# Linear attention and a routed attention layer on one core: the sums over phi(k) taken from three VectorE additions per pair of heads to two, with the rest of them on the array, and the order drawn up anew

## The chip, the cores and the metric

The kernel runs on one core of one Trainium2 chip. The core has five engines that run in parallel, each through its own list of instructions in order: TensorE (PE, with its weight loads PEld), VectorE (DVE), ScalarE (ACT), GpSimd (POOL) and SyncE (SP), which issues nearly all DMAs. The metric is the device time of one execution in microseconds; before the change it is 621.88 us (median of 3 runs, 620.62 to 622.17).

## What is computed

The reference is a linear attention, whose output goes through a layer that routes each token to two of four causal attentions:

```python
def phi(x):
    proj = np.einsum('bhsd,df->bhsf', x, w_phi)
    proj = proj - np.max(np.abs(proj), axis=-1, keepdims=True)
    return np.concatenate([np.exp(proj), np.exp(-proj)], axis=-1)
q_p, k_p = (phi(q), phi(k))
kv = np.einsum('bhsf,bhsd->bhfd', k_p, v)
z = np.sum(k_p, axis=2)
num = np.einsum('bhsf,bhfd->bhsd', q_p, kv)
den = np.einsum('bhsf,bhf->bhs', q_p, z)[..., None] + 1e-06
return (num / den)
...
for e in range(E):          # 4 experts, head size 64, S = 576, 2 of 4 per token
    q = x @ wq[e]; k = x @ wk[e]; v = x @ wv[e]
    ...                     # causal softmax a of q k^T / 8
    out += mask * w * ((a @ v) @ wo[e])
```

There are 8 batches, 8 heads, 576 positions, head size 64 and 128 features (256 with both signs). The change touches z, the sum of phi(k) over the 576 positions.

## The kernel before, in words

The work goes by **pairs** of heads, 32 of them (four to a batch), and by batches for the routed layer. For a pair, the k projection (`stream_k`, L509, nine matmuls, array in two halves of 64 rows) leaves nine blocks of 128 positions by 128 features in PSUM: four whole chunks of each head, and one block that holds the last 64 positions of both. `center` takes the maximum of each position on VectorE (L564) and subtracts it into the tile `ek` (L578); ScalarE makes the exponentials of both signs (L326). `ek` is then 128 positions x 2 signs x 9 blocks x 128 features.

`stream_kv` multiplies phi(k) with v (L605, twenty f32 matmuls, the array in four column tiles of 32, four at a time) and then makes z in the same PSUM tile (L622): a matmul whose weights are ones adds a block of phi(k) up over its positions. For the four pairs of the first batch all five blocks of a head go to the array. For the other 28 pairs `key_sum` (L542) first adds the four whole chunks of each head on VectorE, in three additions of 512 columns (L546), each of them over both signs and both heads, into the tile `zs` (128 x 2 signs x 2 heads x 128); the array then takes `zs` with ones (one round of four matmuls, 2 heads x 2 signs) and the shared block with `sel` (another round).

On the other side, `stream_q` projects q (L509), ScalarE copies the result out (u, L324), GpSimd takes the maximum over features (L681), VectorE subtracts it (L685), ScalarE makes both exponentials. `stream_n` makes the denominators (L710) and numerators (L721), `divide` the quotients x in two parts xh and xl (L753, L324, L319). When a batch's four pairs are through, `stream_s` projects queries and keys of the experts (L315, qk), makes scores (L838), GpSimd masks (L942) and takes maxima (L959), VectorE subtracts (L963), ScalarE exponentiates; `stream_v` makes values and gates (L315 vg, L924), `sums` the softmax denominators (L1001), `attend` the weighted values (L1030), `project_out` the output (L315 wo), which leaves through two tiles `ot` and a store per tile.

Nothing of this order is left to the hardware. Every step is a generator that says which engine it wants and what it needs; the loop of `Plan` picks at each moment the step with the lowest position among those that could start within WINDOW of the earliest, with positions from the tables MOVE, POS1, POS and BOFF, and costs for engines that could take a copy (`copies`, FLEX). Each engine's list is fixed by that. PSUM is eight tiles of 128 x 512 in one pool. While nothing is due at the start, TensorE is given matmuls on a constant tile (`warm`).

The lines that matter below: KADD (L46) is the number of VectorE additions' form; L544 to L551 are the two forms; L610 to L622 let the array take one partial sum per head and sign (`first` = 1) or two.

## Time and profile before

| what | value |
|---|---|
| median of 3 runs | 621.88 us (620.62 to 622.17) |
| the profiled execution's own time | 620.78 us |
| its span, first to last instruction | 619.0 us |
| PE / PEld busy | 607.7 us (98%) / 477.7 us (77%) |
| DVE busy | 541.4 us (87%), 1115 instructions |
| ACT busy | 424.2 us (69%), 1011 instructions |
| POOL busy | 246.0 us (40%) |
| mean granted TensorE clock | 0.998 |

The profiled execution is one run of its own: 1.8 us of its time lie outside the span, and it is 1.1 us below the median of the three runs. "Busy" of PE counts matmuls until their modelled ends, which overlap the next ones. Engines not named in the table (SP, the DMA queues) only move data.

### The profile page before, as it was taken

Reading aid. Unit: us, or ns where it says so; the run is one execution under the profiler, and the core shown is the slowest. Engines: PE = TensorE matmul, PEld = TensorE weight load, DVE = VectorE, ACT = ScalarE, POOL = GpSimd, SP = SyncE. Lnnn points to the kernel's source line nnn. Section 1 sums busy time; section 2 is a strip of 40 time slices with the busy share of each in tenths; the row PEclk is TensorE's granted clock in tenths of the full one; section 3 lists DMA queues with packets and bytes.
Section 4 is the critical chain, followed back from the end, with each engine's and each line's share of the span. In section 5 each row is a group of like instructions: output and inputs, shape, how many; then the busy total and the mean of one; then the engine's idle time right before and its main releaser. Section 6 shows DMA issues by size and latency. Waiting matters only on the chain.

```text
span 619.0 us, 20200 instructions
## 1 busy us (share of the span) xinstructions
PE 607.7 (98%) x8391; PEld 477.7 (77%) x8391; DVE 541.4 (87%) x1115; ACT 424.2 (69%) x1011; POOL 246.0 (40%) x167
## 2 busy tenths in 40 slices
PE   8999999999999999999999999999999999999996
PEld 7656888677896779767886778876789678877985
DVE  5899989999989997989999998789995899976693
ACT  4997769379565796569766867565867478753562
POOL 5644352284332644253445223345152336320520
PEclk9999999999999999999999999999999999999999
DMA  8653214333133431351314242144222311020012
GB/s 219 168 137 95 64 36 122 85 105 87 46 107 90 116 90 33 93 155 55 90 52 140 66 143 62 41 138 119 59 70 92 82 47 28 21 84 2 1 60 96
DMA packets 41611, 52.50 MB, mean 85 GB/s; under 512 B 21168, under 2 KB 24624, under 8 KB 41520
## 3 DMA queue, kind: packets, MB, share of 16 engines
q1 hardware_dynamic: 41200, 50.62, 28.1%
q8 instruction: 66, 1.08, 0.7%
q10 hardware_dynamic: 320, 0.59, 0.4%
q14 instruction: 25, 0.20, 0.1%
HBM read 36.64 MB, written 14.55 MB: 83 GB/s over the span
## 4 chain that ended last, share of the span: by engine, by line
PE 77%; DVE 11%; ACT 9%; issue 1%; DMA 1%; ACTq 0%; DVEq 0%
PE ps_c L315 32%; PE ps_c L605 9%; PE ps_c L509 9%; PE ps_c L721 7%; PE ps_c L1030 6%; PE ps_c L838 5%; PE ps_c L1001 3%; PE ps_c L710 3%; PE ps_c L622 2%; DVE zs L546 2%; ACT ek L326 2%; ACT u L324 2%; ACT mx L326 1%; DVE u L685 1%; DVE top L955 1%
## 5 line engine op out<-in xcount | busy, mean ns | idle before, releaser
L681 POOL PARTITION_ALL_REDUCE mx<-u x64 | 143.7, 2288 | 191.6 <-ACT u L324 188.7
L315 PE MATMUL ps_c<-xh,qk 128*128 128x320 f32 (+1 forms) x512 | 106.5, 299 | 1.8 <-DVE xl L319 1.0
L315 PEld LDWEIGHTS ps_c<-xh,qk 128*128 128x128 f32 x512 | 82.8, 188 | 4.4 <-DVE xl L319 1.2
L959 POOL PARTITION_ALL_REDUCE max<-top x16 | 58.8, 3676 | 67.8 <-DVE top L955 61.3
L942 POOL TENSOR_SCALAR_AFFINE_SELECT s<-s 128x256 f32<-128x256 f32 (+1 forms) x80 | 44.4, 590 | 89.8 <-ACT s L324 89.4
L326 ACT ACTIVATE ek<-ek 128x1152 f32<-128x1152 f32 x64 | 74.8, 1168 | 7.0 <-DVE ek L578 6.3
L605 PE MATMUL ps_c<-ek,v_in 128*32 128x256 f32 x1280 | 75.4, 380 | 0.9 <-ACT ek L326 0.9
L315 PE MATMUL ps_c<-xl,qk 128*128 128x256 f32 (+1 forms) x256 | 75.6, 295 | 0.0
L963 DVE TENSOR_TENSOR s<-s,max 128x1152 f32<-128x1152 f32 (+4 forms) x80 | 68.2, 880 | 4.9 <-POOL max L959 4.9
L685 DVE TENSOR_TENSOR u<-u,mx 128x576 f32<-128x576 f32 x64 | 60.9, 959 | 2.2 <-POOL mx L681 2.2
L605 PEld LDWEIGHTS ps_c<-ek,v_in 128*32 128x32 f32 x1280 | 40.2, 110 | 28.4 <-ACT ek L326 1.2
L315 PE MATMUL ps_c<-vg,xh 128*128 128x260 f32 (+1 forms) x320 | 59.0, 285 | 0.2 <-ACT s L324 0.2
L326 ACT ACTIVATE s<-s 128x1152 f32<-128x1152 f32 (+4 forms) x80 | 56.3, 739 | 3.6 <-DVE s L963 3.4
L564 DVE TENSOR_REDUCE pmax<-ps_c 128x4 f32<-128x512 f32 (+1 forms) x96 | 49.7, 542 | 8.2 <-PE ps_c L509 7.9
L324 ACT COPY s<-ps_c 128x512 f32<-128x512 f32 (+4 forms) x136 | 48.0, 460 | 8.9 <-PE ps_c L838 8.9
L315 PE MATMUL ps_c<-yh,wo 128*128 128x320 f32 (+1 forms) x256 | 52.8, 301 | 0.0
L324 ACT COPY u<-ps_c 128x320 f32<-128x320 f32 (+1 forms) x126 | 41.3, 411 | 15.6 <-PE ps_c L509 15.3
L326 ACT ACTIVATE mx<-u 128x576 f32<-128x576 f32 x64 | 44.0, 689 | 10.2 <-DVE u L685 10.0
L578 DVE TENSOR_TENSOR ek<-ps_c,pmax 128x512 f32<-128x512 f32 (+1 forms) x96 | 50.3, 540 | 0.2 <-PE ps_c L605 0.2
L315 PEld LDWEIGHTS ps_c<-vg,xh 128*128 128x128 f32 (+1 forms) x320 | 47.5, 177 | 1.3 <-ACT s L324 0.5
L315 PEld LDWEIGHTS ps_c<-xl,qk 128*128 128x128 f32 x256 | 48.2, 188 | 0.0
L509 PEld LDWEIGHTS ps_c<-wf,k_in 64*128 64x128 f32 x576 | 41.7, 191 | 8.0 <-DVE u L336 1.0
(119 smaller groups left out, 1379.3 us busy)
## 6 DMA issues: line engine op xcount, KB each, us to landing
v_in<-in_v_dram SPq DMA_DIRECT2D x32, 320.0 KB, 3.0
out_dram<-ot SPq DMA_DIRECT2D x32, 288.0 KB, 2.1
q_in<-in_qt_dram SPq DMA_DIRECT2D x60, 144.0 KB, 2.9
kvd<-kvt SPq DMA_DIRECT2D x104, 48.0 KB, 1.9
kv<-kvd SPq DMA_DIRECT2D x26, 192.0 KB, 2.5
k_in<-in_kt_dram SPq DMA_DIRECT2D x32, 144.0 KB, 2.8
k_in<-in_kt_dram SPq DMA_DIRECT2D x32, 128.0 KB, 2.7
q_in<-in_qt_dram ACTq DMA_DIRECT2D x4, 144.0 KB, 3.7
```

What stands on the lines that cost most here:

```text
L315: nc.tensor.matmul(o, a, b, start=start, stop=stop, skip_group_check=True)
L324: nc.scalar.copy(o, i)
L326: nc.scalar.activation(o, i, func, **kw)
L509: nc.tensor.matmul(o, a, b, start=True, stop=True, skip_group_check=True)
L564: dve(n * 128, [mk], [pk]).tensor_reduce(out=m[:, us], in_=src, axis=AX.X, op=ALU.max, apply_absolute_value=True)
L578: dve(n * 128, [e1k], [pk, mk]).tensor_tensor(out=ek2[p % EKB][:, 1, us, :], in0=src, in1=m[:, us].unsqueeze(2).to_broadcast([128, n, 128] ...
L605: nc.tensor.matmul(o[g, 0:2], v_in[:, 4 * h + t if t < 4 else 8 + h, k:64:2], ek[:, :, u_, :].rearrange("p c (w f) -> p c w f", w=4), star ...
L681: nc.gpsimd.partition_all_reduce(M, U, 128, bass_isa.ReduceOp.absmax)
L685: (nc.gpsimd if st.eng == 'POOL' else nc.vector).tensor_tensor(out=U, in0=U, in1=M, op=ALU.subtract)
L942: nc.gpsimd.affine_select(out=d, in_=d, pattern=[[0, 2], [1, w]], compare_op=ALU.is_ge, fill=FILL, base=0, channel_multiplier=-1)
L959: nc.gpsimd.partition_all_reduce(big.rearrange("p e s -> p (e s)"), top.rearrange("p e s -> p (e s)"), 128, bass_isa.ReduceOp.max)
L963: dve(2 * (S - 128 * j), [('d', x, j)], [('max', z)], 1.11, True).tensor_tensor(out=block(s_, j, None, rows(j)), in0=block(s_, j, None, ro ...
```

## The change

It sets KADD from 3 to 1, so that the second form of `key_sum` is used: for each sign one addition of 512 columns, chunks 0 and 1 of both heads plus chunks 2 and 3, into `zs` of twice the size; two additions per pair in place of three, and neither needs the other. The array takes two rounds of ones in place of one, and the `sel` round as before. All numbers that set the order and the choice of engine for a copy are other ones, too; a line of each kind stands here for the tables.

```diff
-HOT = 16.28
-SLOPE = (-37.28, -27.25, 9.68, 3.86, -6.2)
+HOT = 26.86
+SLOPE = (-74.83, -35.32, -26.8, 10.28, 10.22)
...
-KADD = 3
+KADD = 1
...
-FLEX = (447, -293)
+FLEX = (341, -272)
...
-WINDOW = 52.0
-SWITCH = 22.0
+WINDOW = 236.0
+SWITCH = 55.0
...
-ZEROS = 25.27
+ZEROS = 59.21
...
-BOFF = (-2.11, 8.18, 6.82, 2.05, 1.07, 6.82, 22.72, -5.5)
+BOFF = (-13.16, -1.84, 3.91, 19.47, 4.04, -0.92, 16.38, -56.14)
...
-OTHER = 12.77
+OTHER = 19.72
```

Two lines of the planner (in `key_sum` and `phi_q`) add FLEX[1] to a cost of GpSimd; they concern KPOOL and PSUB, which are 0 in both, so they change nothing.

The code that KADD picks, the same in both files:

```python
for a in range(1, 4 if KADD == 3 else 1):
    ...tensor_tensor(out=zs, in0=zs if a > 1 else x[:, :, :, 0], in1=x[:, :, :, a], op=ALU.add)
for c in range(0 if KADD == 3 else 2):
    ...tensor_tensor(out=zs[:, c], in0=x[:, c, :, 0:2], in1=x[:, c, :, 2:4], op=ALU.add)
```

How the order moves, at three places. The **key sum**, on TensorE, at the pair 17 (`ek` and `v_in` are its phi(k) and v; a row that ends in x20 stands for twenty matmuls). Before:

```order
L710 MATMUL ps_c_68<-u_132,kv_120 32x288
L605 MATMUL ps_c_70<-ek_109,v_in_107 32x2x4x32 x20
L622 MATMUL ps_c_70<-zs,ones 32x4x32 x4
L622 MATMUL ps_c_70<-ek_109,sel 32x4x32 x4
L721 MATMUL ps_c_67<-mx_139,kv_120 32x256 x2
L721 MATMUL ps_c_67<-mx_140,kv_120 32x256 x2
```
With the change:

```order
L710 MATMUL ps_c_66<-u_126,kv_119 32x288
L605 MATMUL ps_c_68<-ek_109,v_in_107 32x2x4x32 x20
L622 MATMUL ps_c_68<-zs,ones 32x4x32 x8
L622 MATMUL ps_c_68<-ek_109,sel 32x4x32 x4
L721 MATMUL ps_c_67<-mx_133,kv_119 32x256 x2
L721 MATMUL ps_c_67<-mx_134,kv_119 32x256 x2
```
The round of ones over `zs` has become two rounds; it still stands right behind the product with v. The same sum on VectorE, at the pair 4, the first that has one. Before:

```order
L753 TENSOR_TENSOR ps_c_65<-ps_c_65,xf 128x256
L753 TENSOR_TENSOR ps_c_68<-ps_c_68,xf 128x320
L546 TENSOR_TENSOR zs<-ek_108 128x512
L546 TENSOR_TENSOR zs<-zs,ek_108 128x512 x2
L319 TENSOR_TENSOR xl_148<-ps_c_65,xh_147 128x256
L319 TENSOR_TENSOR xl_148<-ps_c_68,xh_147 128x320
```
With the change:

```order
L336 COPY kvt<-ps_c_65 128x384
L551 TENSOR_TENSOR zs<-ek_108 128x512
L753 TENSOR_TENSOR ps_c_66<-ps_c_66,xf 128x256
L551 TENSOR_TENSOR zs<-ek_108 128x512
L319 TENSOR_TENSOR xl_146<-ps_c_66,xh_145 128x256
L753 TENSOR_TENSOR ps_c_63<-ps_c_63,xf 128x320
```
Three additions have become two, and a step of another kind stands between them.

The **start**, on ScalarE (`ek_108` is phi(k) of the first pair, `mx` and `u` are phi(q), `qk` a weight). Before:

```order
L324 COPY u_128<-ps_c_66 128x320
L326 ACTIVATE mx_134<-u_126 128x576
L326 ACTIVATE ek_108<-ek_108 128x1152 x2
L326 ACTIVATE mx_133<-u_125 128x576
L326 ACTIVATE mx_136<-u_128 128x576
L326 ACTIVATE u_128<-u_128 128x576
L324 CAST qk<-top_155 128x1152
L326 ACTIVATE u_125<-u_125 128x576
```
With the change:

```order
L324 COPY u_128<-ps_c_66 128x320
L326 ACTIVATE ek_108<-ek_108 128x1152 x2
L326 ACTIVATE mx_134<-u_126 128x576
L326 ACTIVATE u_126<-u_126 128x576
L326 ACTIVATE mx_135<-u_127 128x576
L326 ACTIVATE u_127<-u_127 128x576
L326 ACTIVATE ek_109<-ek_109 128x1152
L324 COPY kvt<-ps_c_66 128x384
```
The first pair's two exponentials of k come ahead of any of q; before, one of q stood ahead of them. On TensorE, 51 matmuls on the constant tile stand ahead of the second k projection in place of 75, and 87 in all in place of 117.

The **tail**, on ScalarE (the copies of the last batch's output tiles; `ot_171` takes the tiles 0 and 2, `ot_172` the tiles 1 and 3). Before:

```order
L324 CAST yh_169<-ps_c_64 128x320
L324 COPY ot_171<-ps_c_68 128x256
L324 COPY ot_171<-ps_c_70 128x320
L324 COPY ot_172<-ps_c_66 128x256
L324 COPY ot_172<-ps_c_64 128x320
L324 COPY ot_171<-ps_c_67 128x256
L324 COPY ot_172<-ps_c_65 128x256
```
With the change:

```order
L324 CAST yh_169<-ps_c_64 128x320
L324 COPY ot_171<-ps_c_69 128x256
L324 COPY ot_172<-ps_c_68 128x256
L324 COPY ot_171<-ps_c_67 128x320
L324 COPY ot_172<-ps_c_66 128x320
L324 COPY ot_171<-ps_c_65 128x320
L324 COPY ot_172<-ps_c_63 128x256
```
The first two tiles are now filled in turns, their first parts before their second ones; VectorE has the two other copies in both, the 320 of tiles 2 and 3 before, the 256 of tile 2 and the 320 of tile 3 now.

Over the whole lists, TensorE has 28 rounds of four matmuls more (112 instructions) and changes the shape of its array tiles 154 times in place of 164. VectorE loses 28 additions and gains 16 copies out of PSUM or of weights that ScalarE had; ScalarE loses these 16.

## Rows read from the trace of the kernel before

**Rows 1.** The page of the profile: its first line, the busy time of the engines over the whole span (microseconds, share of the span, instructions), and the shares by engine of the chain of work that ended last.
```profile
span 619.0 us, 20200 instructions
...
PE 607.7 (98%) x8391; PEld 477.7 (77%) x8391; DVE 541.4 (87%) x1115; ACT 424.2 (69%) x1011; POOL 246.0 (40%) x167
...
PE 77%; DVE 11%; ACT 9%; issue 1%; DMA 1%; ACTq 0%; DVEq 0%
```

**Rows 2.** Busy time of each engine in three stretches (start and end in us from the span's start, length, then busy us of each engine with its instructions, granted TensorE clock as a share of full speed, DMA share, GB/s): the ramp of the first batch, the middle, the last two batches and the tail.
```profile
0.00:62.00 62.00, 58.92 (x886) 40.72 (x888) 52.60 (x109) 49.19 (x99) 31.91 (x21) 1.00 0.58 155
62.00:530.00 468.00, 464.92 (x6433) 365.77 (x6433) 426.76 (x870) 327.80 (x780) 192.52 (x128) 1.00 0.29 83
530.00:619.00 89.00, 83.84 (x1084) 71.17 (x1075) 62.08 (x137) 47.22 (x133) 21.58 (x19) 0.99 0.13 46
```

**Rows 3.** The TensorE timeline around one pair's key sum (start us, us until the modelled end of the last one, engine, line, operation, out<-in, array tile, shape, records; an f32 matmul leaves two records, so x8 is one round of four).
```profile
101.74 0.43 PE L622 MATMUL ps_c<-zs,ones 128*32 128x128 f32 x8
101.98 0.40 PE L622 MATMUL ps_c<-ek,sel 128*32 128x128 f32 x8
102.20 1.54 PE L1001 MATMUL ps_c<-s,ones 128*32 128x288 f32 x40
```

**Rows 4.** Groups of instructions with shapes kept apart (line, engine, operation, out<-in, shapes, count; busy us, mean ns of one; idle us of the engine just before them and what ended it): the key sum's additions, a copy of VectorE out of PSUM, and the steps between a k projection and its exponentials.
```profile
L546 DVE TENSOR_TENSOR zs<-zs,ek 128x512 f32<-128x512 f32 x56 | 43.8, 783 | 0.9
...
L546 DVE TENSOR_TENSOR zs<-ek 128x512 f32<-128x512 f32 x28 | 21.2, 757 | 2.5 <-PE ps_c L622 1.5 <-ACT ek L326 0.9
...
L336 DVE COPY ot<-ps_c 128x320 f32<-128x320 f32 x13 | 6.4, 489 | 11.1 <-DMA out_dram<-ot 8.3 <-PE ps_c L315 2.2 <-ACT ps_c L326 0.5
...
L578 DVE TENSOR_TENSOR ek<-ps_c,pmax 128x512 f32<-128x512 f32 x64 | 41.8, 674 | 0.2 <-PE ps_c L605 0.2
...
L564 DVE TENSOR_REDUCE pmax<-ps_c 128x4 f32<-128x512 f32 x64 | 41.4, 675 | 8.2 <-PE ps_c L509 7.9
...
L326 ACT ACTIVATE ek<-ek 128x1152 f32<-128x1152 f32 x64 | 74.8, 1168 | 7.0 <-DVE ek L578 6.3
```

**Rows 5.** The TensorE timeline in two places (columns as in rows 3): the second round of L710 followed by a step of another tile shape, and followed by one of the same.
```profile
23.33 0.67 PE L710 MATMUL ps_c<-u,kv 128*32 128x288 f32 x8
...
23.93 0.38 PE L509 MATMUL ps_c<-wf,k_in 64*128 64x128 f32 x2
...
111.01 0.67 PE L710 MATMUL ps_c<-u,kv 128*32 128x288 f32 x8
...
111.49 0.38 PE L605 MATMUL ps_c<-ek,v_in 128*32 128x256 f32 x1
```

**Rows 6.** The start: rows of the timelines of TensorE, of VectorE and of ScalarE (columns as in rows 3; in brackets the idle time before the row and what ended it).
```profile
10.23 4.36 PE L315 MATMUL ps_c<-warm 128*128 128x128 bf16 x75
...
14.52 1.39 PE L509 MATMUL ps_c<-wf,k_in 64*128 64x128 f32 x18
...
16.28 2.37 PE L605 MATMUL ps_c<-ek,v_in 128*32 128x256 f32 x40
...
11.72 0.75 DVE L685 TENSOR_TENSOR u<-u,mx 128x576 f32<-128x576 f32 x1
...
12.39 0.28 DVE L578 TENSOR_TENSOR ek<-ps_c,pmax 128x128 f32<-128x128 f32 x1
...
12.50 0.68 ACT L326 ACTIVATE mx<-u 128x576 f32<-128x576 f32 x1 [1.40 <-DVE u L685]
...
13.09 2.34 ACT L326 ACTIVATE ek<-ek 128x1152 f32<-128x1152 f32 x2
```

**Rows 7.** The tail: rows of the timelines of TensorE, of VectorE and of ScalarE, and last one piece of the chain of work that ended last (start us, us, what).
```profile
608.45 0.46 PE L315 MATMUL ps_c<-yh,wo 128*128 128x320 f32 x2
...
608.89 0.40 PE L315 MATMUL ps_c<-yh,wo 128*128 128x256 f32 x2
...
609.25 0.45 PE L315 MATMUL ps_c<-yh,wo 128*128 128x320 f32 x2
...
609.59 0.49 DVE L319 TENSOR_TENSOR yl<-ps_c,yh 128x320 fp32r<-128x320 f32 x1 [0.49 <-ACT yh L324]
...
615.21 0.49 DVE L336 COPY ot<-ps_c 128x320 f32<-128x320 f32 x1 [0.36 <-DMA out_dram<-ot]
...
611.25 1.66 ACT L324 COPY ot<-ps_c 128x256 f32<-128x256 f32 x4 [1.69 <-PE ps_c L315]
...
615.13 0.37 ACT L324 COPY ot<-ps_c 128x256 f32<-128x256 f32 x1 [0.42 <-DMA out_dram<-ot]
...
612.93 2.10 DMA out_dram<-ot
```

**Rows 8.** Waits of TensorE's weight loads from 20 to 606 us (engine, out and line, what was waited for: us in total, times, longest us).
```profile
PEld ps_c L315 <- DVE xl L319: 1.6, 2, 1.2
...
PEld ps_c L509 <- DVE ps_c L753: 1.4, 3, 0.5
...
PEld ps_c L509 <- ACT mx L326: 1.4, 4, 0.5
...
PEld ps_c L605 <- ACT ek L326: 1.2, 2, 1.1
```

**Rows 9.** The TensorE timeline of the fourth pair: its k projection, and the step that multiplies its phi(k) with v (columns as in rows 3).
```profile
36.58 1.39 PE L509 MATMUL ps_c<-wf,k_in 64*128 64x128 f32 x18
...
45.60 0.64 PE L605 MATMUL ps_c<-ek,v_in 128*32 128x256 f32 x8 [0.86 <-ACT ek L326]
```

More of the change, by code (lines that the diff above doesn't have):

```diff
@@ L91 @@
-POS1 = {'wq': 7.17, 'wv': 21.48, 'wo': 24.58, 'n0': -30.0, 'n1': 2.78, 'k': -0.6, 'q': -13.78, 'v': -0.62, 'kv': -23.5, 'z': 3.8, 'cen': -4.87, 'evu': -35.73, 'ph0': 17.23, 'ph1': 17.65, 'div': -1.88, 'evd': -4.7, 'lk': -16.22, 'lq': 24.67}
-BOFF = (-2.11, 8.18, 6.82, 2.05, 1.07, 6.82, 22.72, -5.5)
-POS = {'fin': 39.8, 'p0': -3.53, 'p1': -40.28, 'v0': 21.78, 'gate': -24.77, 's0': -7.94, 's1': -10.44, 'm0': 9.16, 'm1': 14.32, 't0': -27.77, 't1': 0.1, 'out': 21.12}
[10 rows of a table added]
+    'evu': (6.8, -21.35, 6.41, -12.3, 7.4, 4.82, 5.05, -0.04, 5.64, -5.01, 5.49, 0.81, -18, -5.64, -22.38, 32.72, 17.12, -0.64, 33.16, 0.57, 12.47, -7.98, 2.62, -2.4, -19.71, 6.85, 3.73, 18.44, -22.69, 4.87, 5.04, -8.19,),
@@ new lines @@
+    'ph0': (12.06, 7.25, 8.9, -8.48, 13.11, 3.32, 23.51, 1.63, 5.19, 11.75, 1.44, 8.87, 7.87, 7.86, 11.54, 0.87, 4.08, -7.89, -0.79, -9.77, -9.31, 16.55, 14.79, 11.86, 9.9, 18.66, 2.49, -3.93, -11.7, -2.14, -14.68, 3.55,),
+    'ph1': (-7.2, -5.86, 14.43, 15.66, 0.79, -6.91, -0.21, 34.16, -10.58, 14.08, -26.56, -3.97, 5.79, -11.42, -2.79, 10.67, -6.73, 1.11, 5.61, -9.25, 2.64, -19.41, 6.71, 7.18, 1.87, 1.45, 1.84, 9.05, -0.28, 4.61, 5.76, -20.17,),
+    'cen': (-1.2, 3.62, -17, 0.94, -20.47, -6.74, 12.4, 4.64, -21.77, -36.49, -10.6, -25.81, -4.54, 6.27, -0.76, -1.9, 2.73, 13.05, 2.8, 9.13, -4.33, 10.79, 7.22, 12.38, 5.9, 11.33, -17.03, 22.59, -14.89, 15.82, -5.18, -7.13,),
@@ new lines @@
+    'evd': (0.41, 19.08, 30.39, 1.01, -20.32, -6.41, -5.63, -1.44, -15.71, 10, 2.66, -3.13, -0.96, 11.86, 4.83, -20.58, 5.65, 3.13, -3.27, -13, -2.84, 29.11, 23.04, 12.83, 0.44, 6.26, -11.11, 5.77, 11.32, 6.98, 0.21, 3.72,),
+    'n1': (3.76, -5.22, -7.46, 11.91, -10.85, 11.23, -18.4, 15.11, 1.37, -11.71, -10.88, -34.34, -3.24, -5.5, 15.08, -3.48, -14.77, -7.9, 5.38, 4.69, 14.84, -19.32, 19.63, 2.43, -13.85, 1.6, -11.58, 0.76, 2.28, -11.93, -16.19, -8.16,),
+    'div': (-8.63, 10.36, 12.6, 18.11, 18.3, -14.25, 5.79, -11.2, 13.01, -0.95, 14.74, -1.86, -16.45, -1.7, -11.92, 0.01, 20.01, 8.27, -10.23, -14.06, 22.17, 1.47, -24.38, 7.08, -1.85, 1.44, -5.84, 6.27, 5.79, -4.31, -7.71, -22.39,),
[6 rows of a table added]
@@ new lines @@
+    'gate': (31.69, -9.55, 4.05, -17.81, 18.54, 8.24, -6.2, 2.69,),
+    't1': (5.02, -0.41, 3, -7.78, 9.18, 15.59, -16.96, -12.72,),
+    'out': (12.41, 3.63, 9.76, 4.79, -6.99, 6.66, -2.08, -6.03,),
+    'fin': (0, 0, 0, 0, 0, 0, 0, -8.63,),
+}
+POS1 = {'wq': 50.59, 'wv': 25.6, 'wo': 36.27, 'n0': -37.41, 'n1': -2.16, 'k': 5.88, 'q': -19.68, 'v': -2.9, 'kv': -22.69, 'z': -14.51, 'cen': -33.17, 'evu': -85.86, 'ph0': 14.95, 'ph1': 12.23, 'div': -32.98, 'evd': -15.7, 'lk': -14.98, 'lq': 23.34}
+BOFF = (-13.16, -1.84, 3.91, 19.47, 4.04, -0.92, 16.38, -56.14)
@@ L95 @@
+POS = {'fin': 20.1, 'p0': 11.95, 'p1': -47.3, 'v0': 19.99, 'gate': -9.45, 's0': 11.63, 's1': 1.85, 'm0': 35.05, 'm1': 7.89, 't0': -12.14, 't1': 0.91, 'out': 23.79}
 NPAIRS = B * NP
@@ L547, in key_sum @@
         for c in range(0 if KADD == 3 else 2):
-            st = Step((('POOL', KPOOL), ('DVE', 65 + 1.11 * 512)) if KPOOL else 'DVE', ekk, pred=has('kv', p - 1) if p else None, port=True)
+            st = Step((('POOL', KPOOL + FLEX[1]), ('DVE', 65 + 1.11 * 512)) if KPOOL else 'DVE', ekk, pred=has('kv', p - 1) if p else None, port=True)
             yield st
```

13 lines of the change are left out of this document (1 added, 12 removed), and 32 rows, old and new, of the table MOVE.

## The prediction

> **What bounds the kernel now.** I read the page first. TensorE is busy for 607.7 of 619.0 us and 77% of the chain that ended last runs over it; VectorE follows with 87% busy and 11% of the chain [rows 1]. A share of busy time alone proves little, so I cut the span into stretches. In the middle, from 62 to 530 us, TensorE shows 464.9 busy of 468 us, at the full granted clock (1.00, the 2.4 GHz level): 3.1 us of visible idle time in three quarters of the run [rows 2]. The reader should see two things there: whatever is added to TensorE's list in that stretch has almost no hole to fall into, and VectorE, 426.8 of 468 us busy, still has 41 us of holes. Losses are outside: the ramp, where constant matmuls fill the wait [rows 6], and the tail, where the last copies wait for a store [rows 7]. All 28 key sums that change lie in or at the edge of the middle.
>
> **The change part by part.**
>
> *More rounds on TensorE.* A round of four matmuls over `zs` starts at 101.74, the round of `sel` at 101.98, the next step at 102.20 [rows 3]. The durations in the rows (0.43, 0.40) overlap; the cost is from start to start, 0.24 and 0.22. The added round stands between its like, so 28 x 0.22 = 6.2 us, all of it on the path, since the middle is full. Bounds: 28 x 0.22 = 6.2 and 28 x 0.24 = 6.7. I take **+6.2**.
>
> *Fewer changes of the array's shape.* The second round of L710 takes 23.93 - 23.33 = 0.60 us when a step of another shape follows and 111.49 - 111.01 = 0.48 when one of the same does [rows 5]: 0.12 per change. Ten changes fewer: 10 x 0.12 = 1.2; I take **-1.1**, as one or two may stand where TensorE waits anyway (bounds 0 and -1.2).
>
> *The start.* Today the first pair's phi(k) meets v at 16.28. The exponentials ran from 13.09 to 15.43, because one of q went ahead of them at 12.50, and because VectorE did one subtraction of q (0.75 us, at 11.72) before the last centring, which ended at 12.67 [rows 6]. In the new lists both stand behind. The exponentials can begin at 12.67 - 0.75 = 11.9 and end at 14.3; the constant matmuls end about 24 x 0.057 = 1.4 us earlier (4.29 us from 10.23 to 14.52 for 75 is 0.057 each), and with the k projection (1.35) and three more the product starts near 14.7. That is 1.6 us sooner. ScalarE, which leads the ramp afterwards, has the same work to do, so some of it is lost again: **-1.0**, bounds 0 and -1.6.
>
> *The tail.* Output tile 3 goes into the buffer of tile 1 and waits for its store: ScalarE's fourth copy ends at 612.91, the store takes 2.10, and the last copy ends at 615.21 + 0.49 = 615.70 [rows 7]. In the new order the first two tiles are finished in turns. The 256 triples cost 0.36 (608.89 to 609.25), those of 320 about 0.44 (608.45 to 608.89). From the first triple on, tile 1's last triple is then over near 611.2 (it may not start before 610.08, when the yl of 320 is made), its copy near 611.8, its store near 613.9, while the last triple of all still ends near 613.8. The last copy would end near 614.5: **-1.2**, bounds 0 and -1.4.
>
> *VectorE's additions.* 28 additions leave; the 84 of today take 43.8 + 21.2 = 65.0 us, 0.774 each, so 21.7 us. Sixteen copies come back to it at about 0.49 each: 7.8 [rows 4]. VectorE has 13.9 us less, ScalarE 16 copies less. Not one of these microseconds is on the path itself; what they are worth is the waiting of TensorE that they shorten. With 427 us busy against 41 idle in the middle, a step that arrives finds VectorE occupied for long stretches; with 413 against 55 the relation falls from 10.4 to 7.5, by 28%. The weight loads' waits with a known producer begin with four kinds that add up to 1.6 + 1.4 + 1.4 + 1.2 = 5.6 us [rows 8], in front of the qk projection, the projections of k and q, and the product of phi(k) with v. The new list puts more between producer and consumer at the first of these: with steps priced as in rows 3 and 5, five of the eight batches now have 4.4 us or more of other TensorE work between the last numerators and qk, where one had. Bounds: nothing, if those waits are replaced by others as long; 9, if the 3.1 visible us and all four kinds go. I take **-5.5**, close to the four kinds, because it is there that the list was loosened.
>
> *The sum.* 6.2 - 1.1 - 1.0 - 1.2 - 5.5 = -2.6 us: span 616.4, own time 620.8 - 2.6 = 618.2. The median of the runs shown is 1.1 above the profiled execution, so the forecast is **619.3 us**, 0.4% faster. A measurement of this kernel can tell about 0.3%, 1.9 us, from no change; the forecast is only just outside, and the last term decides.
>
> **The rivals.**
>
> *The waits shrink only half as much.* Relief of 2.8 in place of 5.5 gives +0.1: 622.0 us, no difference. For it: most waits in the list are single ones of half a microsecond, and a chain VectorE to ScalarE to VectorE keeps its length however free VectorE is. Against it: the loosened places.
>
> *The relief was hidden anyway.* TensorE takes its 6.2 us and gets back only what start, tail and shape changes give: 6.2 - 1.1 - 1.0 - 1.2 = +2.9, 624.8 us. From a relief under 1.0 us on, the result is slower by over 0.3%. For it: 3.1 us of visible idle time is all that the middle shows.
>
> *phi(k) comes late for v* (slower as well). The place is the wait of L605 for the exponentials. Behind a k projection VectorE needs 2 x 0.675 + 2 x 0.674 and two small steps of 0.28, ScalarE 2 x 1.17 [rows 4]: 5.6 us without any queue, and with one the fourth pair needed 45.60 - 37.97 = 7.6 and made TensorE wait 0.86 [rows 9]. In the old list three pairs have under 7.6 us of TensorE work in between, in the new one eleven, three of them only 5.5. The shortfalls of the new list against 7.6 add up to some 11 us, those of the old one to 3. If half of the difference of 8 is waited for, the forecast becomes 623.3; all of it, 627.3. It decides from 4.5 us up. Against it: with fewer additions VectorE's queue is shorter just there.
>
> *TensorE is not full.* The weight loads are busy for only 77%, so the added rounds might slip in between [rows 1]. Then the 6.2 us fall away: 613.1 us. Against it: the middle's 3.1 us of idle time, and rounds that follow each other at a fixed 0.22 to 0.24. The Trainium skill, Perfetto Trace Analysis, section Identifying the Most-Contended Engine, holds that the busy share of matmuls is a poor measure of how full TensorE is and that the busy share of weight loads should be read instead; by that rule there would be room for a quarter more. The start-to-start times in the trace do not bear it out for these steps.
>
> That the change might not do what it says can be left out: the lists show the additions and rounds as described.
>
> **How the numbers follow.** Forecast 0.40 (619.3); TensorE not full 0.07 (613.1); half the relief 0.27 (622.0); relief hidden 0.15 (624.8); phi(k) late 0.11 (623.3 to 627.3). So faster 0.47, within 0.3% 0.27, slower 0.26. The forecast's own range runs from 615.8 (relief 9) to 620.0. The range for 8 in 10 must take in half the relief and the hidden relief and most of the late phi(k), and on the low side half of the not-full case: **613.5 to 626.0**.
>
> **What would show it.** Rounds of L622 over `zs` at 0.22 each, 56 in place of 28; VectorE near 528 us busy; the first L605 near 14.7 us; the last copy of the output under 1 us behind the last matmul; PEld's waits on `xl` gone. The prediction is wrong if the middle's visible idle time grows, above all in front of L605 after `ek`, or if the four kinds of waits come back under other names.

## The result: 627.33 us, slower by 0.94%

The changed kernel takes 627.33 us (median of 4 runs, 626.81 to 627.82) against 621.8 for the kernel before beside it: a ratio of 1.0094, 95% interval 1.0081 to 1.0107. The forecast was 619.3 us; the time lies above its range. The profiled execution is one of 627.32 us with a span of 625.5.

### The profile page after: what moved, and what is told of

It is laid out like the page before. It is cut to its first block, busy times and chain, and to the rows that moved or that the text cites. A ratio compares the mean times of both kernels' runs of the same rounds, so it can differ in the third digit from the quotient of the medians.

```text
span 625.5 us, 20541 instructions
## 1 busy us (share of the span) xinstructions
PE 610.8 (98%) x8585; PEld 480.3 (77%) x8585; DVE 535.6 (86%) x1103; ACT 422.7 (68%) x995; POOL 239.2 (38%) x167
## 4 chain that ended last, share of the span: by engine, by line
PE 78%; DVE 10%; ACT 7%; issue 2%; DMA 1%; POOL 1%; SPq 0%; DVEq 0%
PE ps_c L315 30%; PE ps_c L509 9%; PE ps_c L605 9%; PE ps_c L721 8%; PE ps_c L1030 6%; PE ps_c L838 6%; PE ps_c L710 4%; PE ps_c L622 3%; PE ps_c L1001 3%; DVE u L685 2%; ACT u L326 1%; ACT ek L326 1%; ACT mx L326 1%; DVE s L963 1%; DVE top L955 1%
## 5 line engine op out<-in xcount | busy, mean ns | idle before, releaser
L681 POOL PARTITION_ALL_REDUCE mx<-u x64 | 142.0, 2269 | 190.8 <-ACT u L324 190.8
L315 PE MATMUL ps_c<-xh,qk 128*128 128x320 f32 (+1 forms) x512 | 106.0, 298 | 0.0
L959 POOL PARTITION_ALL_REDUCE max<-top x16 | 57.8, 3615 | 77.6 <-DVE top L955 41.0
L315 PEld LDWEIGHTS ps_c<-xh,qk 128*128 128x128 f32 x512 | 82.7, 188 | 1.6 <-ACT xh L324 0.4
L326 ACT ACTIVATE ek<-ek 128x1152 f32<-128x1152 f32 x64 | 74.7, 1167 | 11.5 <-DVE ek L578 10.9
L605 PE MATMUL ps_c<-ek,v_in 128*32 128x256 f32 x1280 | 75.4, 381 | 1.8 <-ACT ek L326 1.7
L315 PE MATMUL ps_c<-xl,qk 128*128 128x256 f32 (+1 forms) x256 | 75.6, 295 | 0.0
L942 POOL TENSOR_SCALAR_AFFINE_SELECT s<-s 128x256 f32<-128x256 f32 (+1 forms) x80 | 39.5, 523 | 93.4 <-ACT s L324 84.5
L963 DVE TENSOR_TENSOR s<-s,max 128x1152 f32<-128x1152 f32 (+4 forms) x80 | 66.1, 858 | 2.8 <-POOL max L959 2.8
L605 PEld LDWEIGHTS ps_c<-ek,v_in 128*32 128x32 f32 x1280 | 39.4, 110 | 30.7 <-ACT ek L326 3.6
L685 DVE TENSOR_TENSOR u<-u,mx 128x576 f32<-128x576 f32 x64 | 59.9, 949 | 0.9 <-POOL mx L681 0.7
L315 PE MATMUL ps_c<-vg,xh 128*128 128x260 f32 (+1 forms) x320 | 58.1, 283 | 0.0
L324 ACT COPY s<-ps_c 128x512 f32<-128x512 f32 (+4 forms) x130 | 45.4, 444 | 16.8 <-PE ps_c L838 16.6
L315 PE MATMUL ps_c<-yh,wo 128*128 128x320 f32 (+1 forms) x256 | 53.1, 302 | 0.0
L315 PEld LDWEIGHTS ps_c<-xl,qk 128*128 128x128 f32 x256 | 48.2, 188 | 0.0
L315 PEld LDWEIGHTS ps_c<-vg,xh 128*128 128x128 f32 (+1 forms) x320 | 47.6, 177 | 0.8 <-issue 0.5
L509 PE MATMUL ps_c<-wf,k_in 64*128 64x128 f32 x576 | 45.6, 284 | 2.5 <-ACT u L324 1.2
```

The source lines that it names most:

```text
L315: nc.tensor.matmul(o, a, b, start=start, stop=stop, skip_group_check=True)
L324: nc.scalar.copy(o, i)
L326: nc.scalar.activation(o, i, func, **kw)
L509: nc.tensor.matmul(o, a, b, start=True, stop=True, skip_group_check=True)
L605: nc.tensor.matmul(o[g, 0:2], v_in[:, 4 * h + t if t < 4 else 8 + h, k:64:2], ek[:, :, u_, :].rearrange("p c (w f) -> p c w f", w=4), star ...
L681: nc.gpsimd.partition_all_reduce(M, U, 128, bass_isa.ReduceOp.absmax)
```

## The profile after

The page of the changed kernel: first line, busy time by engine, shares of the chain that ended last by engine.

```profile
span 625.5 us, 20541 instructions
...
PE 610.8 (98%) x8585; PEld 480.3 (77%) x8585; DVE 535.6 (86%) x1103; ACT 422.7 (68%) x995; POOL 239.2 (38%) x167
...
PE 78%; DVE 10%; ACT 7%; issue 2%; DMA 1%; POOL 1%; SPq 0%; DVEq 0%
```

Against [rows 1] VectorE's busy time fell by 5.8 us and the span grew by 6.5. The forecast had VectorE at 528 us, 13.9 less: the durations of its instructions, added up, did fall by 13.8 (from 608.3 to 594.6), but they overlap, and the busy time counts each moment once. The span minus TensorE's busy time, 11.3 us before, is 14.7 now: TensorE has more work and waits more, too. The stretches of [rows 2] show where (columns as there):

```profile
0.00:62.00 62.00, 56.86 (x875) 39.84 (x879) 50.28 (x108) 45.55 (x90) 31.25 (x21) 0.97 0.62 158
62.00:530.00 468.00, 463.03 (x6546) 362.82 (x6536) 417.46 (x847) 326.64 (x769) 182.21 (x123) 1.00 0.29 83
530.00:625.00 95.00, 90.90 (x1177) 77.64 (x1175) 67.88 (x150) 50.51 (x136) 25.71 (x25) 1.00 0.12 43
```

In the middle VectorE is busy for 9.3 us less, and yet TensorE's visible idle time rose from 3.1 to 5.0 us. That is the sign which the prediction named for being wrong.

The additions and the rounds are as announced. The group of the additions, with that of the exponentials and the first maxima from [rows 4], and a TensorE timeline around one key sum, as in [rows 3]:

```profile
L551 DVE TENSOR_TENSOR zs<-ek 128x512 f32<-128x512 f32 x56 | 44.8, 815 | 2.7 <-PE ps_c L622 2.0 <-ACT ek L326 0.5
...
L326 ACT ACTIVATE ek<-ek 128x1152 f32<-128x1152 f32 x64 | 74.7, 1167 | 11.5 <-DVE ek L578 10.9
...
L564 DVE TENSOR_REDUCE pmax<-ps_c 128x4 f32<-128x512 f32 x64 | 41.3, 681 | 12.2 <-PE ps_c L509 11.9
```

```profile
422.11 0.62 PE L622 MATMUL ps_c<-zs,ones 128*32 128x128 f32 x16
422.55 0.40 PE L622 MATMUL ps_c<-ek,sel 128*32 128x128 f32 x8
422.76 0.62 PE L721 MATMUL ps_c<-mx,kv 128*32 128x256 f32 x8
```

Two rounds take 422.55 - 422.11 = 0.44 us, 0.22 each, as the prediction had them. But ScalarE now waits 10.9 us for the subtractions of VectorE before its exponentials (6.3 before).

The weight loads' waits from 20 to 606 us, as in [rows 8]:

```profile
PEld ps_c L509 <- ACT u L324: 4.9, 6, 1.4
PEld ps_c L605 <- ACT ek L326: 3.6, 5, 1.5
PEld ps_c L509 <- DVE xl L319: 2.2, 4, 1.3
```

The wait of L315 on `xl`, 1.6 us before, is gone. A wait of L509 on `xl` has come, that of L605 on `ek` trebled, and the waits of the projections for ScalarE's copy of `u` are the new first. At the two places of the middle where TensorE stood longest, the chains behind these names end on VectorE. The timelines of VectorE and GpSimd, and of TensorE, at 107 to 113 us:

```profile
107.14 1.97 DVE L913 TENSOR_TENSOR gs<-gs,tiny 128x5 f32<-128x5 f32 x1
...
112.03 0.49 DVE L319 TENSOR_TENSOR xl<-ps_c,xh 128x320 fp32r<-128x320 f32 x1 [0.29 <-ACT xh L324]
...
106.99 3.58 POOL L959 PARTITION_ALL_REDUCE max<-top  x1 [6.13 <-DVE gt L911]
...
112.57 0.70 PE L509 MATMUL ps_c<-q_in,wf 64*128 64x256 f32 x2 [0.87 <-DVE xl L319]
```

An addition of 5 columns, which takes 0.17 us elsewhere, took 1.97 because it began 0.15 us after a reduction of GpSimd. All of VectorE's list behind it moved by 1.8 us, and the q projection waited for a PSUM tile until its last reader, the `xl` of L319, was through. The same engines at 422 to 430 us:

```profile
422.78 1.74 DVE L551 TENSOR_TENSOR zs<-ek 128x512 f32<-128x512 f32 x1
...
425.25 2.20 DVE L551 TENSOR_TENSOR zs<-ek 128x512 f32<-128x512 f32 x1
427.37 0.47 DVE L732 STREAM_TRANSPOSE widey<-ps_c 128x288 f32<-128x288 f32 x1
...
424.72 3.66 POOL L959 PARTITION_ALL_REDUCE max<-top  x1
...
427.88 0.83 ACT L326 ACTIVATE ps_c<-widey 64x9 f32<-64x9 f32 x4 [2.14 <-DVE widey L732]
...
429.84 1.38 PE L509 MATMUL ps_c<-wf,k_in 64*128 64x128 f32 x16 [1.15 <-ACT u L324]
```

Here the two additions of the new form, 0.68 us each undisturbed, took 1.74 and 2.20. The transpose behind them was late, ScalarE waited 2.14 us for it and did its copy of `u` late, and the k projection waited for the PSUM tile that this copy frees. The wait is named after ScalarE; the loss arose on VectorE.

## What the runs tell apart

Each group of kernels ran on one chip, in turns with the kernel before, and every ratio is to that. Shares of a ratio are turned into microseconds with 621.3; a difference of two ratios is uncertain by 1.1 to 1.3 us.

Where two traces are laid side by side, instruction by instruction, the first 13 us are left out of the comparison: executions with the same lists differ there. In the traces of the two kernels and of the versions below in which the first product of phi(k) with v reads phi(k), that product begins at 13.4 to 15.8 us in the seven with the new lists and at 15.1 to 17.0 in the nine with the old ones.

### Prices in the exact order of either kernel

The first four keep every engine's list as it is and leave out, or double, single instructions.

e3, the new order without the second round:

```diff
+                        if adds and t == 1:
+                            continue
                         nc.tensor.matmul(o[g:g + 32, 2], a_, ...
```

> The changed kernel in its own order, without the second of the two rounds of ones on TensorE (28 pairs, 4 matmuls each); the sum over k of phi(k) thus lacks half of its chunks. Theory A (TensorE is full, each added round costs its whole 0.22 us wherever it stands, and what VectorE was spared brings nothing): 28 x 0.22 = 6.2 less, 621.1, between 620.3 and 622. Rival B (the rounds lie partly in TensorE's waits, and the time went to the new order): 3 less or fewer, 624 to 627.

Measured: 622.01 us, ratio 1.0010 (1.0002 to 1.0019). From 1.0094 that is 5.2 us for 28 rounds, 0.19 each. The rounds cost nearly their full length. In the two profiled executions TensorE's list gains only 2.8 us behind the start, since 1.7 us are lost from 114 us on: there the granted clock of e3 stood at the lower of its two levels for 3.4 us, behind two waits of 0.9 and 1.0 us after which it stayed at 1.00 in the change. Without that loss it would be 4.5, by this estimate. And the new order, freed of every added round and with 28 additions fewer on VectorE, is no faster than the kernel before.

e4, the old order with its round emitted twice:

```diff
+                        for again in range(2 if adds and t == 0 else 1):
-                        nc.tensor.matmul(..., start=t == 0, ...
+                            nc.tensor.matmul(..., start=t == 0 and again == 0, ...
```

> The kernel before in its own order, with its one round of ones emitted twice for 28 pairs (the sums of the first eight chunks count twice in it); VectorE's three additions stay. A: 621.8 + 6.2 = 628.0, between 627 and 629. B: the rounds find idle time in the old order, 625 or less.

Measured: 625.79 us, ratio 1.0073 (1.0057 to 1.0088): 4.5 us, between the two. With both traces side by side, each round sets TensorE's list back by 0.2 to 0.26 where it stands; some 0.25 us each come back at nine places (62, 142, 152, 192, 222, 346, 424, 516 and 534 us), where TensorE waited anyway.

e5, the old order with one of three additions:

```diff
+            if a == 1:
                 ....tensor_tensor(out=zs, in0=..., in1=x[:, :, :, a], op=ALU.add)
```

> The kernel before in its own order, of the three additions of phi(k) per pair only the first is carried out (56 additions of 0.69 us fewer, 39 us of VectorE; the sum lacks chunks). A: VectorE bounds little, the waits of TensorE that end on VectorE in the middle are worth 1 to 2 us: 621.8 - 1.5 = 620.3, between 619 and 622. Rival C (the relief works as I forecast, 5.5 us for 14 us of VectorE, and is lost in the new order only): 616 or less.

Measured: 618.38 us, ratio 0.9950 (0.9937 to 0.9962): 3.1 us for 39 us of VectorE (36 by its busy time), 0.08 per us, a little more than A expected and far from C. The gain comes in steps of 0.3 to 0.9 us at few places (62, 142, 152, 222, 346, 430 and 534 us), 0.3 are lost again at 192 and at 284, and between them the two traces run in parallel.

e6, the new order without its additions:

```diff
         plan.run(st.eng, ..., ['zs'], ekk, ...)
+        if p > 4:
+            continue
         (...).tensor_tensor(out=zs[:, c], in0=x[:, c, :, 0:2], in1=x[:, c, :, 2:4], op=ALU.add)
```

> The changed kernel in its own order, without the two additions of phi(k) in all pairs but the first that has them (54 additions of 0.68 us fewer, 37 us of VectorE; the partial sums are those of one pair throughout). A: VectorE's share of the waits in the new order is small too: 627.3 - 2, between 624 and 627. Rival D (the new order waits because VectorE is late, above all where its additions ran 1 to 1.5 us longer beside GpSimd): 623 or less.

Measured: 623.2 us, ratio 1.0035 (1.0023 to 1.0047): 3.7 us less than the change, between A and D: 0.10 per us of VectorE. By itself that is not clearly more than the 0.08 of e5; e17, below, is the fair counterpart.

### Form and order apart

e8 puts the form of the change into the places of the old order:

```diff
-            dve(...).tensor_tensor(out=zs, in0=zs if a > 1 else x[:, :, :, 0], in1=x[:, :, :, a], op=ALU.add)
+            if a < 3:
+                add.tensor_tensor(out=zs[:, a - 1], in0=x[:, a - 1, :, 0:2], in1=x[:, a - 1, :, 2:4], op=ALU.add)
...
+                        for half in range(2 if adds and t == 0 else 1):
+                            if adds and t == 0:
+                                x_ = zs[:, c, h, half]
```

> The form of the change (two additions to partial sums, two rounds of ones) put into the places of the old order: the two additions stand where the first and second of the three stood, the third place is empty, the second round stands behind the first. Everything is computed. Theory A2 (prices add: the rounds cost 4.6 in the old order, as their doubling did, and VectorE's relief pays 2.9 for 39 us, so 1.4 for these 28 additions of 0.69): 621.2 + 4.6 - 1.4 = 624.4, between 623.5 and 625.5; what the change measures beyond that, some 2.7, is then the new order. Rival B2 (the order is innocent, the form alone costs all of it): 626.5 to 628. Rival C2 (the relief pays here what I forecast, 5.5): 620 to 621.5.

Measured: 624.26 us, ratio 1.0045 (1.0031 to 1.0058), as A2 has it. **The form alone costs 2.8 us** (rounds 4.5, relief -1.7), **and the new order 3.0 more**, the last two uncertain by 1.3 and 1.2. The middle of e8, against 463.03 busy and 5.0 idle in the change (columns as in [rows 2]):

```profile
62.00:530.00 468.00, 466.44 (x6555) 372.68 (x6548) 405.33 (x839) 327.21 (x775) 187.48 (x127) 1.00 0.29 83
```

TensorE idles for 1.6 us there, 3.4 less than in the new order: that is where the new order loses, in waits.

e7 is the reverse, the new order with three additions and one round:

```diff
+        nc.vector.tensor_tensor(out=zs[:, :, :, 0], in0=zs[:, :, :, 0], in1=zs[:, :, :, 1], op=ALU.add)
...
+                        if adds and t == 1:
+                            continue
```

> The new order with the old form: behind the second addition a third one joins the two partial sums on VectorE (28 of 0.69 us more there), and TensorE takes the first round only. Everything is computed. A2: 622.0 (without second rounds) + 19.3 us of VectorE at the 3.9 for 37 us that the additions cost in this order = 2.0: 624.0, between 623 and 625, slower than before by the worth of the order, 2 to 3. B2: as before, 621 to 622. A third case (the new order has no room on VectorE where the third addition stands, in front of what TensorE waits for): 626 or more.

Measured: 635.95 us, ratio 1.0252 (1.0228 to 1.0277), the third case: 15.0 us above e3 for 28 additions. The waits of its weight loads (L625 is the round, L841 the scores):

```profile
PEld ps_c L625 <- DVE zs L552: 5.1, 6, 1.3
...
PEld ps_c L509 <- DVE xl L319: 3.7, 3, 2.0
PEld ps_c L841 <- DVE yl L319: 2.7, 1, 2.7
```

Only 5.1 us are the round's own wait for the sum; the rest is VectorE being late for everything behind it. Some 3.4 of the 15.0 us are the clock: in the profiled execution it stood at the lower level twice for 3.4 us (from 116 and 167 us), behind waits of TensorE of 1.0 and 2.2 us, and e3 lost 1.7 in such a stretch.

e1 and e2 turn only the switch of the form and let the other kernel's numbers set an order (`KADD = 1` in the kernel before, `KADD = 3` in the changed one).

> The kernel before with only the switch of the form turned: the old numbers, the planner sets a new order from them. A2: the numbers were fitted to the old form, the order is some other one: the form's 3.2 plus between 0 and 4, 624 to 629. B2: 626.5 to 628. C2: 622 or less.

> The changed kernel with only the switch turned back: the new numbers, three additions and one round, the planner sets a new order. A2: 622 to 627, the new numbers plus the old form, which costs TensorE 28 rounds fewer. B2: the form is all, 621 to 622.

Measured: 653.58 us, ratio 1.0523 (1.0508 to 1.0537), and 638.79, ratio 1.0286 (1.0272 to 1.0300). Both far outside every expectation. Numbers fitted to one form give a bad order for the other, so these two say nothing of the form; e8 and e7 do, since they hold the order.

### The price of VectorE's time upwards

If a round costs 4.5/28 and VectorE's time 0.08 per us, the opposite trade should pay. e11 lets VectorE add the ninth chunk, too, and drops the round of `sel`; e10 does it for every second pair (`range(2 if p % 2 else 0)`).

```diff
+        for h in range(2):
+            r = slice(64 * h, 64 * h + 64)
+            nc.vector.tensor_tensor(out=zs[r, :, h], in0=zs[r, :, h], in1=ek[r, :, 8, :], op=ALU.add)
...
+                        if adds and t == first:
+                            continue
```

> The trade of the change the other way round, in the old order: for the 28 pairs VectorE also adds the ninth chunk (two additions of 64x256 behind the third of 128x512), and TensorE's round with sel (4 matmuls) is left out. Everything is computed. Theory A4 (in the old order a round is worth 4.6/28 and VectorE's time 0.075 us per us): 621.1 - 4.6 + 56 x 0.4 x 0.075 = 621.1 - 4.6 + 1.7 = 618.2, 617 to 619.5, which would be faster than both. Rival B4 (VectorE has no room before TensorE's round, as where the third addition stood in the new order, which cost 14): 622 or more.

> The same for every second pair only (14). Everything is computed. A4: half of 2.9: 619.7, 619 to 620.5. B4: 621.5 or more; a case between, in which VectorE's room is used up by half of it: 619.5 here and 621 or more with all pairs.

Measured: 640.25 us, ratio 1.0308 (1.0289 to 1.0328), and 629.02, ratio 1.0136 (1.0116 to 1.0156). Both are B4, and by far. The group of the added instructions in e11:

```profile
L554 DVE TENSOR_TENSOR zs<-zs,ek 64x256 f32<-64x256 f32 x56 | 30.8, 549 | 1.7
```

19.1 slower, plus the 4.5 that the dropped rounds are worth, is 23.6 us for 30.8 us of VectorE: 0.77 per us, ten times the price downwards. Here, too, the clock has a part: it stood at the lower level for 3.4 us from 196 us and for 6.8 from 326, behind waits of TensorE of 0.9 and 1.9 us. At half speed that is some 5 us, and without them an estimate of 0.6 per us. The rest could be the place, right in front of TensorE's round. e14 adds work that nobody waits for, behind the third addition:

```diff
+    zd = sb("zd", [128, 2, 2, 128])
...
+        nc.vector.tensor_tensor(out=zd, in0=x[:, :, :, 2], in1=x[:, :, :, 3], op=ALU.add)
```

> The kernel before with a fourth addition of 128x512 per pair on VectorE (28 of 0.69 us), behind the third, into a buffer that nobody reads; everything is computed as before. Theory A5 (VectorE's room in the fitted order is gone in one direction: taking work from it pays 0.075 us per us, adding work delays everything that stands behind it, 0.7 to 1 us per us, as with the ninth chunk): 621.3 + 13 to 19, 634 to 640. Rival B5 (only what stands between phi(k) and the round of ones that TensorE takes from it costs, and this addition does not): 621.3 to 624.

Measured: 631.07 us, ratio 1.0153 (1.0138 to 1.0169): 9.5 us, below A5's interval but far from B5. VectorE's busy time rose from 541.4 to 562.4, so 0.45 per us, without any direct reader, and the granted clock stays at 1.00 in the middle. The middle of e14:

```profile
62.00:530.00 468.00, 458.99 (x6270) 358.50 (x6267) 437.35 (x879) 318.69 (x763) 190.84 (x124) 1.00 0.29 83
```

9.0 us of idle time of TensorE, where 3.1 were, with VectorE at 437 of 468.

### Why the new order waits

First the collisions with GpSimd. e9 leaves out the two reductions beside which VectorE was held at 107 and 425 us, e12 two others (`SKIP = (3, 11)`), e18 three (`SKIP = (1, 3, 9)`); e13 leaves two out of e8 (`SKIP = (7, 9)`).

```diff
+SKIP = (1, 9)
...
+        if n not in SKIP:
             nc.gpsimd.partition_all_reduce(big..., top..., 128, bass_isa.ReduceOp.max)
```

> The changed kernel in its own order without two of its sixteen reductions over partitions of the scores' maxima on GpSimd (the second, at 107.0 us, and the tenth, at 424.7 us of its profile; those two blocks of scores are scaled by the maxima of the block before). Beside these two starts VectorE's addition at L913 took 1.97 us in place of 0.17 and one at L551 2.20 in place of 0.68, and TensorE stalled behind them at 111 and 428. Theory A3 (the new order's loss against the old order with the same form, 2.9, is mainly these collisions of VectorE with GpSimd): 627.1 - 1.8 - 1.2 = 624.1, 623.5 to 625.3. Rival B3 (it is the new order as a whole, with VectorE's work close in front of TensorE's everywhere; a delay saved at one place is waited for at the next): 626.3 to 627.3.

Measured: 623.77 us, ratio 1.0044 (1.0031 to 1.0057), 3.1 less than the change. VectorE, and then TensorE, of e9 at the two places (line numbers one higher than in the change):

```profile
106.55 0.17 DVE L914 TENSOR_TENSOR gs<-gs,tiny 128x5 f32<-128x5 f32 x1
...
106.97 0.95 DVE L916 TENSOR_TENSOR col<-gt,gs 128x20 f32<-128x20 f32 x1
...
423.68 0.67 DVE L552 TENSOR_TENSOR zs<-ek 128x512 f32<-128x512 f32 x1
...
426.66 1.46 PE L510 MATMUL ps_c<-wf,k_in 64*128 64x128 f32 x18
```

The small addition takes 0.17 us again (the next reduction now holds another one for 0.95), the second key sum 0.67, and the k projection runs in one piece. TensorE's lists of the two profiled executions differ by 0.6 us before 112 us, which is the start, by 1.6 behind it, and by 3.1 from 430 us on; between the two places nothing changes. So the two places gave 1.0 and 1.5 us.

> The changed kernel in its own order without two other of the sixteen reductions of the scores' maxima on GpSimd (the fourth, at 175.8 us, and the twelfth, at 508.7; those blocks are scaled by the maxima of the block before). Beside their starts VectorE took 1.33 us longer at L897 and 1.41 at L685, and no idle time of TensorE follows. Theory A3 (only the two collisions in front of TensorE's stalls cost): 626.9, between 626.3 and 627.5. Rival D3 (any two reductions less speed this order, since each takes 3.6 us of GpSimd and a wait of VectorE with it): 623.5 to 625.

Measured: 625.53 us, ratio 1.0072 (1.0057 to 1.0087), 1.4 less than the change and between the two expectations. A3 looked for a stall right behind the collision only; the trace gains 1.5 us in steps from 187 to 202 us, 11 to 26 us behind the reduction at 175.8, and nothing behind the other.

> The old order with the form of the change (two additions, two rounds; 624.3), without two of the sixteen reductions on GpSimd (the eighth, at 345.4 us, and the tenth, at 419.2; those blocks are scaled by the maxima of the block before). Beside them L685 took 1.49 and 1.58 us longer; TensorE stalls behind the first, not behind the second. Theory A3 (what a collision costs is what TensorE waits behind it): 624.3 less at most 1: 623.2 to 624.2, so that the old order has less of this to lose than the 3.4 of the new one. Rival E3 (both orders lose the same to such collisions, and the difference of 2.9 is something else): 620.5 to 621.5.

Measured: 622.14 us, ratio 1.0008 (0.9998 to 1.0018), 2.3 less than e8: more than A3 allowed. The old order loses to such collisions as well. They are part of the loss in both, and alone don't explain the 3.0.

Next the rival of the prediction, phi(k) late for v: e15 (new order) and e16 (old order, form of the change) let TensorE read a tile that is always ready.

```diff
-                        nc.tensor.matmul(o[g, 0:2], v_in[...], ek[:, :, u_, :]...
+                        nc.tensor.matmul(o[g, 0:2], v_in[...], wf...to_broadcast([128, 2, 4, 32]),
...
-                            a_, x_, r_ = sel[:, h, :], ek[:, c, 8, :], ekk
+                            a_, x_, r_ = sel[:, h, :], wf[:, 0:128], ekk
```

> The changed kernel in its own order; TensorE's kv product (L605) and its round with sel read a weight tile that lies ready in place of phi(k), so that they no longer wait for ScalarE's ek. All other engines do the same work, and the rounds of ones still wait for zs. Theory F (my rival of the prediction: phi(k) is late for TensorE in the new order, 3.6 us of waits before L605 against 1.2): 627.3 - 2.4 or more, 623.5 to 625. Rival G (the late phi(k) is only where VectorE's lateness shows; TensorE then waits for zs or a PSUM buffer instead): 626 to 627.5.

> The same in the old order with the form of the change (624.3). F: 1.2 us of such waits, 623 to 624, so that 2 or less of the 2.9 between the orders is left. G: 623.5 to 624.5, and 2.5 to 3 are left.

Measured: 626.6 us, ratio 1.0093 (1.0078 to 1.0108), and 624.04, ratio 1.0049 (1.0034 to 1.0064). Neither moved. The 3.6 us of waits on `ek` are gone, and their time is waited for elsewhere. The rival is refuted, although its 627.3 happened to be the time measured.

Last, VectorE's load itself: e17 is e8 without its additions in all pairs but the first that has them (`if a < 3 and p < 5`), the counterpart of e6.

> The old order with the form of the change (two rounds; 624.3), without the two additions in all pairs but the first that has them (54 fewer, 37 us of VectorE; the counterpart of e6, which gained 3.9 in the new order). Theory H (what sets the orders apart is how close VectorE's work stands in front of TensorE's; with the additions gone the new order has its room back and the 2.9 between them shrinks): 624.3 - 1.5 = 622.8, 622.2 to 623.3, against the 623.2 to 623.4 of e6. Rival I (the gap is in the order of TensorE itself or its PSUM buffers): 620 to 621.3, 2 to 3 below e6.

> The changed kernel in its own order without the second, fourth and tenth reductions on GpSimd (e9's two and the one of e12's in whose wake TensorE gained; those blocks are scaled by the maxima of the block before). H: the places add, 2.5 + 1.6 by the two traces: 623.2 to 623.4 minus another 1 to 1.7, 622 to 622.7. Rival: the stall saved by one is waited for at the next, 623.3 to 624.

Measured: e17 623.0 us, ratio 1.0030 (1.0016 to 1.0043), e18 622.41, ratio 1.0016 (1.0005 to 1.0028). With the additions the orders are 3.0 us apart; without them 0.3, with an uncertainty of about 1 (e6 1.0035, e17 1.0030). The middle of e6, and then of e17:

```profile
62.00:530.00 468.00, 465.30 (x6569) 366.63 (x6561) 385.45 (x798) 329.00 (x777) 183.92 (x128) 1.00 0.29 83
...
62.00:530.00 468.00, 467.16 (x6615) 374.55 (x6619) 372.67 (x783) 327.86 (x776) 184.72 (x127) 1.00 0.29 83
```

TensorE's idle time falls from 5.0 to 2.7 us in the new order and from 1.6 to 0.8 in the old one. Behind the start its list gains 4.6 us in e6, in four steps (186 to 202, 268 to 272, 374 to 376 and 428 to 430 us), and 1.1 us in e17. The first and the last of the four are also places where e12 and e9 gain by leaving out a reduction of GpSimd: VectorE is late there, and either two additions fewer per pair or one reduction fewer helps. TensorE's waits that name `zs` itself add up to only 0.4 us in the change, so it isn't the sum being late for its own round. So the gap between the orders is VectorE's lateness in the new one, as far as the uncertainty lets it be told. And the collisions add up: three reductions less give 4.8 us by the medians, and the trace has 4.1 of it in steps at 112, 187 to 202 and 430 us. The two traces differ by another 2.4 us in the start; how much of the remaining 0.7 comes from there is not shown.

None of these versions beats the kernel before with the whole computation in it.

## Why the prediction was wrong

| term | forecast | measured |
|---|---|---|
| rounds on TensorE | +6.2 | +4.5 (e4, old order), +5.2 (e3, new order) |
| VectorE's relief | -5.5 | -1.7 (e8 against e4, old order) |
| order: shape changes, start, tail | -1.1 -1.0 -1.2 | +3.0 together (e8 against the change) |
| sum | -2.6 | +5.8 |

**The rounds** were right in kind and 1 to 1.7 too dear: 0.22 each in its place, of which TensorE's existing waits take back a part. The rival that TensorE is not full is refuted. The Trainium skill, Perfetto Trace Analysis, section Identifying the Most-Contended Engine, wants TensorE's headroom judged by the achieved share of peak operations (MFU, not worked out here) and the busy share of weight loads; read alone, weight loads at 77% would mean room. e4, with 78%, pays for most of the length of its rounds, so the measurement decides against that reading here.

**The relief is the step that failed**, in both of its halves. First its size: I took the four kinds of waits of TensorE that name VectorE or ScalarE, 5.6 us, as what a freer VectorE would give back, because its ratio of busy to idle time fell by 28%. But a list in fixed order doesn't behave like a queue with an average wait. Relief pays where TensorE in fact waits for VectorE, in e5 at seven places, and nothing between; the price down is 0.08 us per us (e5), 0.03 to 0.10 over all versions (e17, e6). I also read only one side: work added to VectorE costs 0.45 (e14) to 0.77 (e11). With VectorE at 91% of the middle, a delay is carried on until the next gap, and there are few.

Second its ground: the full 5.5 was taken because the new list was loosened at some places, and the waits did not shrink in the new list but grew, from 1.6 us of visible idle time in the middle of e8 to 5.0. The sum missed by 8.4 us: the rounds cost 1.7 less than forecast (by e4), the relief in the old order is short by 3.8, and the new order is off by 6.3. Of the 6.3 start and tail explain at most 1.5 and the shape changes at most 1.1; the rest is waiting that no term of the sum foresaw. The rivals, too, took the three terms of the new order as gains, and only the late phi(k) reached 627 at its far end.

**The order** was forecast as a gain by three small terms. The shape changes can't be priced alone in these runs. The start gave 0.45 us between the two profiled executions, but over all the traces compared above the first product begins 1.0 us earlier with the new lists (15.0 against 16.0 in the mean), with a spread of some 2 us within each group: the term was about right. TensorE and ScalarE in the change, as in [rows 6], and the first stretches (granted clock third from the right):

```profile
14.24 1.39 PE L509 MATMUL ps_c<-wf,k_in 64*128 64x128 f32 x18
...
15.83 2.37 PE L605 MATMUL ps_c<-ek,v_in 128*32 128x256 f32 x40
...
12.47 2.36 ACT L326 ACTIVATE ek<-ek 128x1152 f32<-128x1152 f32 x2 [0.33 <-DVE ek L578]
...
5.00:10.00 5.00, 3.89 (x29) 3.42 (x31) 0.57 (x1) 1.31 (x4) 2.14 (x1) 0.74 0.99 249
10.00:15.00 5.00, 5.00 (x71) 4.43 (x69) 4.70 (x8) 3.90 (x7) 3.10 (x2) 0.92 1.02 204
```

In this execution the exponentials began at 12.47 and not at 11.9, and ended at 14.83; the product then waited for the k projection in front of it on TensorE's own list, over at 15.6. The tail, as in [rows 7]:

```profile
620.60 0.31 PE L315 MATMUL ps_c<-yl,wo 128*128 128x320 f32 x1
...
621.79 0.49 DVE L336 COPY ot<-ps_c 128x320 f32<-128x320 f32 x1 [0.33 <-DMA out_dram<-ot]
...
618.93 2.67 DMA out_dram<-ot
```

The last copy ends 621.79 + 0.49 - 620.91 = 1.37 us behind the last matmul, 1.66 before: 0.3 gained here and 0.5 in six of the seven other traces with the new lists (1.1 us), not 1.2, since it still waits for the buffer's store, which took 2.67 us here. What outweighs these gains is VectorE's work standing closer in front of TensorE's: 5.0 against 1.6 us of idle time in the middle, and a loss of 3.0 us that shrinks to 0.3 when VectorE's additions are gone (e6, e17). That the prediction saw no such price has the same root as the failed step: it read the loosened places of the new list and set against them only one tight one, phi(k), which e15 shows to be harmless.

What stays open: the new order's gains in start, tail and shape changes should show as 1 to 2 us once the additions are gone, and e6 against e17 shows 0.3 in the other direction; the uncertainty of about 1 doesn't decide that, and e6 still idles for 1.9 us more in the middle. How much of e9 is the held additions and how much the reductions' own time on GpSimd is not separated either, though the rows put TensorE's two steps right behind the held instructions.

## What to carry to other kernels

An engine at 90% in front of a full one has two prices: taking work from it pays only at the few places where the full engine waits for it (0.03 to 0.10 us per us here), adding work costs 0.45 to 0.8, the upper end with waits long enough that TensorE's granted clock fell behind them. So price relief by those single waits, one by one, never by the busy share; and read a new order for what stands directly in front of the full engine, with the longest times that the producers take and not their medians. To tell form from order, put the new form into the old list by hand; a planner that runs again on foreign numbers changes everything at once (18 to 32 us here).
